# Attention and MLP on one core: 444 matmuls without use behind the last real one

## The chip, the cores and the metric

The kernel runs on one core of one Trainium2 chip. The metric is the device time in microseconds (us) of one execution. Its engines are PE (TensorE, matrix multiply), ACT (ScalarE), DVE (VectorE), POOL (GpSimd) and SP (SyncE, which issues transfers). PEld is PE's loading of weights. SBUF is the on-chip memory of 128 partitions from which operands are read; PSUM holds what PE writes, in eight banks of 512 f32 columns per partition.

## The reference

Windowed attention with 32 global positions, and behind it an MLP with an exact GELU, in f32:

```
s_ll = where(|i - j| <= 32, scale * q_l k_l^T, -1e9);  s_lg = scale * q_l k_g^T
out_l = softmax([s_lg, s_ll]) @ [v_g, v_l]
out_g = softmax(scale * q_g [k_g, k_l]^T) @ [v_g, v_l]
x = concat([out_g, out_l]) as (B * 544, 512)      # B = 8, 8 heads of 64, 512 local positions
h = x @ w_in                                       # 512 x 2048
out = (0.5 * h * (1 + erf(h / sqrt(2)))) @ w_out   # 2048 x 512
```

The output has 4352 rows of 512.

## The kernel before, in words

The 4096 local rows are done in 16 chunks of 256 (a batch element and a half of its positions), and the 256 global rows of all batch elements in a 17th, with the key "g". For each chunk the attention of four pairs of heads comes first, then the MLP of the chunk. So that products come out in f32 accuracy at the faster operand type, an operand is split in a high part (rounded to fp32r) and a low part (the rest), and three matmuls, high by high, low by high and high by low, are added in PSUM.

Names and lines that matter here:

- `wh[n]` and `wl_[n]` are the high and low parts of the weights, 128 x 512 each, for n = 0 to 31: even n is a block of `w_in` (four column blocks of 128, one for each 128 inputs), odd n one of `w_out`. They stay in SBUF. High parts lie two in a tile of 1024 columns, low parts have tiles of their own.
- `st["xh", key, c]` and `st["xl", key, c]` are the parts of the chunk's input, 128 x 256, c = 0 to 3.
- `ml_hc` (lines 709 to 711) makes a hidden block of a chunk: for each c three matmuls with a stationary weight block of 128 x 128 and 256 moving columns, into a PSUM tile of the pool `ps_h`, tag "h", which has two banks.
- `ml_g`, `ml_gh`, `ml_gl` do the GELU (line 279, ACT) and split its result into `gh` and `gl` (lines 132, 134 and 139).
- `ml_o` (lines 744 to 746) multiplies them with `w_out`: three matmuls of 512 moving columns for each block and each of two accumulators.
- `ml_e` and `ml_w` copy an accumulator to SBUF (line 132) and send it out (line 759 for key "g").
- `a_ts`, two SBUF tiles of the attention, and `xs`, the chunk's input before it is split, are free when the last chunk's MLP runs.

The functions don't issue instructions where they stand. They are entered as steps in a list with the engine, the time that it takes and the time that it is due; a planner in the kernel's Python then places the steps engine by engine, and the last loop (line 1086) issues them in that order. `behind` ties each instruction to the one before it on its engine, so the order on an engine is the planner's:

```
    for t, i, x in order:
        x["fn"](x["on"], *x["args"])
        ...
        for y in ins[seen:]:
            if y.engine in last:
                behind(y, last[y.engine])
            last[y.engine] = y.name
```

The program ends when that loop has ended. Its last steps are those of key "g": the matmuls of lines 744 to 746, two copies of the accumulators on ACT, and eight transfers, of which SP's queue issues six and ACT's queue two.

Of the kernel before, what the change touches and what calls it, by code (L numbers as in the profile page):

```python
# [8 lines left out]
F32 = mybir.dt.float32  # L9
# [4 lines left out]
AF = mybir.ActivationFunctionType  # L14
# [70 lines left out]
def attn_mlp(ctx, tc, q_l, k_l, v_l, q_g, k_g, v_g, w_in, w_out, out):  # L85
# [1000 lines left out]
    for t, i, x in order:  # L1086
# [14 lines left out]
            taker[kind] = ins[seen].name, ins[seen].engine  # L1101
        seen = len(ins)


# [1 line left out]
_INS = ['q_l', 'k_l', 'v_l', 'q_g', 'k_g', 'v_g', 'moe_w_in', 'moe_w_out']  # L1106
# [26 lines left out]
```

## Time and profile before

| what | us |
|---|---|
| median of 2 runs | 1052.23 (1052.16 to 1052.3) |
| profiled execution | 1050.12 |
| its span, from the first to the last instruction | 1048.3 |
| PE busy | 1016.1 (97%) |
| ACT busy | 676.9 (65%) |
| DVE busy | 680.4 (65%) |
| POOL busy | 380.4 (36%) |

The granted clock of TensorE is 1.000 on average over the span. The profile is of one execution; its times count from the first instruction. In a row of the timeline stand the start, the duration, the engine, the line of the code, the operation, and the result and operands by their names in the program. A matmul is pipelined: the next one starts long before its record ends, so what a matmul costs in a stream is the step from one start to the next. A row of a group has, behind the count, the sum of the busy time, the mean duration in ns, and the idle time before. A row of windows gives for each engine the busy time and, in brackets, the number of instructions, then the granted clock, the share of the transfer engines that was in use, and GB/s.

### The profile page before, as it was taken

The page shows a single profiled execution, that of the slowest core. Times are in us where ns is not written, and L with a number is a line of the kernel's source. Part 1 is how long each engine was busy: PE and PEld are TensorE (multiplying, and loading weights), DVE is VectorE, ACT ScalarE, POOL GpSimd, SP SyncE. Part 2 cuts the span into 40 slices and gives each one's busy share as a digit, 9 for nine tenths or more (in the row PEclk, how much of TensorE's full clock was granted, in tenths as well). Part 3 has the DMA queues.
Part 4 walks back from the last instruction along what each step waited for, and adds up shares of the span by engine and source line. Part 5 has one row for each costly group of instructions (what it writes and reads, how often), then busy time and mean ns, then how long its engine had stood idle before and what let it go on. Part 6 is the DMA issues. An engine that isn't in the chain of part 4 may idle for free.

```text
span 1048.3 us, 21420 instructions
## 1 busy us (share of the span) xinstructions
PE 1016.1 (97%) x7000; PEld 903.3 (86%) x7000; DVE 680.4 (65%) x2089; ACT 676.9 (65%) x1617; POOL 380.4 (36%) x427
## 2 busy tenths in 40 slices
PE   4989999999999999999999999999999999999998
PEld 2756699998988989998999999998999989999897
DVE  2978968667676768677775777577676777561000
ACT  2978886776667766777575666577565766573221
POOL 2111575243332534334342525244333434243121
PEclk9999999999999999999999999999999999999999
DMA  7785332214221233213322332213322332101000
GB/s 186 226 256 201 55 77 45 53 43 81 49 64 30 42 84 65 59 36 60 82 39 56 61 71 59 61 34 76 64 42 51 64 72 59 44 14 56 1 21 21
DMA packets 277983, 72.29 MB, mean 69 GB/s; under 512 B 263152, under 2 KB 271344, under 8 KB 277872
## 3 DMA queue, kind: packets, MB, share of 16 engines
q1 hardware_dynamic: 271792, 68.57, 28.5%
q10 hardware_dynamic: 6080, 2.36, 0.9%
q8 instruction: 55, 0.90, 0.3%
q14 instruction: 56, 0.46, 0.2%
HBM read 61.41 MB, written 9.44 MB: 68 GB/s over the span
## 4 chain that ended last, share of the span: by engine, by line
PE 84%; DMA 4%; ACT 4%; DVE 3%; SPq 3%; issue 1%; POOL 0%; ACTq 0%; DVEq 0%; POOLq 0%
PE h L709 11%; PE h L711 10%; PE h L710 10%; PE acc L744 10%; PE acc L745 10%; PE acc L746 10%; PE o L517 5%; PE s L406 4%; PE t L480 2%; PE acc L736 2%; PE h L705 2%; PE go L650 2%; ACT a_t L279 1%; PE sg L563 1%; DMA wraw<-in_moe_w_in_dram 1%
## 5 line engine op out<-in xcount | busy, mean ns | idle before, releaser
L139 POOL TENSOR_TENSOR gl<-gf,gh 128x512 fp32r<-128x512 f32 x127 | 167.9, 1322 | 406.4 <-ACT gh L132 282.1
L709 PE MATMUL h<-xh,wh 128*128 128x256 f32 x1024 | 299.1, 292 | 1.4 <-ACT gf L279 1.4
L711 PE MATMUL h<-xh,wl 128*128 128x256 f32 x1024 | 289.7, 283 | 0.0
L710 PE MATMUL h<-xl,wh 128*128 128x256 f32 x1024 | 289.3, 283 | 0.0
L744 PE MATMUL acc<-wh,gh 128*128 128x512 f32 x512 | 206.3, 403 | 0.0
L709 PEld LDWEIGHTS h<-xh,wh 128*128 128x128 f32 x1024 | 195.0, 190 | 10.4 <-ACT gf L279 1.8
L745 PE MATMUL acc<-wh,gl 128*128 128x512 f32 x512 | 201.7, 394 | 0.0
L746 PE MATMUL acc<-wl,gh 128*128 128x512 f32 x512 | 200.6, 392 | 0.0
L710 PEld LDWEIGHTS h<-xl,wh 128*128 128x128 f32 x1024 | 195.2, 191 | 5.7 <-issue 0.7
L711 PEld LDWEIGHTS h<-xh,wl 128*128 128x128 f32 x1024 | 195.0, 190 | 0.0
L279 ACT ACTIVATE gf<-h 128x512 f32<-128x512 f32 x136 | 81.1, 597 | 73.2 <-POOL gl L139 37.7
L279 ACT ACTIVATE a_t<-a_t,sm 128x192 f32<-128x192 f32 (+1 forms) x256 | 116.9, 458 | 2.9 <-DVE sm L431 2.0
L746 PEld LDWEIGHTS acc<-wl,gh 128*128 128x128 f32 x512 | 96.4, 188 | 21.6
L425 DVE CUSTOM_DVE_ANT_0 a_t<-s,mask 128x192 f32<-128x192 f32 (+1 forms) x256 | 80.4, 367 | 48.0 <-PE s L406 48.0
L132 ACT ACTIVATE gh<-gf 128x512 fp32r<-128x512 f32 x95 | 60.0, 632 | 77.2 <-PE acc L746 76.1
L744 PEld LDWEIGHTS acc<-wh,gh 128*128 128x128 f32 x512 | 96.9, 189 | 13.0
L745 PEld LDWEIGHTS acc<-wh,gl 128*128 128x128 f32 x512 | 97.0, 189 | 11.3
L500 DVE TENSOR_TENSOR at<-t,at 128x512 fp32r<-128x512 f32 (+1 forms) x112 | 67.7, 618 | 38.7 <-ACT at L132 38.2
L132 ACT ACTIVATE at<-t 128x512 fp32r<-128x512 f32 (+1 forms) x112 | 59.4, 541 | 49.8 <-PE t L481 25.9
L139 POOL TENSOR_TENSOR vs<-vr,vs 128x512 fp32r<-128x512 f32 x56 | 74.8, 1336 | 42.6 <-DVE vs L134 23.9
L279 ACT ACT_TABLE_LOAD x69 | 88.5, 1283 | 1.2
L548 DVE TENSOR_TENSOR xs<-o,xs 64x256 f32<-64x256 f32 x112 | 46.1, 412 | 51.9 <-ACT xs L543 50.6
(132 smaller groups left out, 1730.9 us busy)
## 6 DMA issues: line engine op xcount, KB each, us to landing
wraw<-in_moe_w_out_dram SPq DMA_DIRECT2D x16, 512.0 KB, 7.6
raws<-in_v_l_dram SPq DMA_DIRECT2D x64, 128.0 KB, 2.5
out_dram<-ob SPq DMA_DIRECT2D x32, 256.0 KB, 2.1
raws<-in_k_l_dram SPq DMA_DIRECT2D x224, 36.0 KB, 1.9
vr<-in_v_l_dram SPq DMA_DIRECT2D x113, 64.0 KB, 2.2
wraw<-in_moe_w_in_dram SPq DMA_DIRECT2D x14, 512.0 KB, 7.4
raws<-in_q_l_dram SPq DMA_DIRECT2D x224, 32.0 KB, 1.8
raws<-in_v_g_dram SPq DMA_DIRECT2D x128, 16.0 KB, 1.9
```

Source lines behind the costliest of these rows:

```text
L132: nc.scalar.activation(out=out, in_=in_, func=AF.Copy)
L139: (nc.vector if e == "v" else nc.gpsimd).tensor_sub(**kw)
L279: nc.scalar.activation(func=func, **kw)
L425: nc.vector.tensor_tensor_reduce(out=a_t[:, j, aoff[half][i]:aoff[half][i] + w], in0=s[:, c:c + w], in1=masks[half][i], scale=1.0, scalar= ...
L500: nc.vector.tensor_sub(out=at[:, 1], in0=st.pop((u, "t", j))[:, :n * P].rearrange("p (n q) -> p n q", q=P), in1=at.bitcast(F32)[:, 0])
L517: nc.tensor.matmul(out=o[:, :, qsl], lhsT=l.rearrange("p s e -> p (s e)"), rhs=r, start=(n == 0), stop=(n == 3), skip_group_check=True)
L709: nc.tensor.matmul(out=h, lhsT=hi, rhs=xh, start=(c == 0 and not (key == (0, 0) and f < HQ and f % 2)), stop=False, skip_group_check=True)
L710: nc.tensor.matmul(out=h, lhsT=hi, rhs=xl, start=False, stop=False, skip_group_check=True)
L711: nc.tensor.matmul(out=h, lhsT=lo, rhs=xh, start=False, stop=(c == NCC - 1), skip_group_check=True)
L744: nc.tensor.matmul(out=acc[t], lhsT=gh[:, f % 2, tsl], rhs=hi, start=(f == 0), stop=False)
L745: nc.tensor.matmul(out=acc[t], lhsT=gl[:, f % 2, tsl], rhs=hi, start=False, stop=False)
L746: nc.tensor.matmul(out=acc[t], lhsT=gh[:, f % 2, tsl], rhs=lo, start=False, stop=(f == NF - 1))
```

## The change

Behind the last loop the changed kernel issues three kinds of instructions more, and ties them to the end of each engine's order in the same way (`after_all`). No line of before is altered, and the order of what stands before is the same.

- `traffic(18)` issues 18 copies of 480 columns on ACT and 18 on DVE, from `xs` into the two tiles of `a_ts`.
- `real(f)`, called four times, issues the twelve matmuls of one hidden block of key "g" once more, into a fresh bank of the pool `ps_h`.
- `run(a, b, n, w, A, B, pre)` issues n equal matmuls into a fresh bank: the stationary block is the 128 columns of B from b on, the moving operand the w columns of A from a on (w is 256 where nothing is given, A the high part of block 2, B the low part of block 3). With `pre` a single matmul with so many columns goes ahead of them.

The calls go through moving operands shifted by 16 columns (and by 4, 8 and 12), stationary blocks shifted by 16 or 32, other pairs of tiles, 512 columns, a single matmul of another width ahead, and other widths. Every matmul starts a new sum, so each overwrites what the one before wrote in its bank, and nothing reads these banks. The output is that of before. The diff:

```diff
+    def after_all(e0):
+        ins = nc.cur_bb.bb.instructions
+        for y in ins[e0:]:
+            if y.engine in last:
+                behind(y, last[y.engine])
+            last[y.engine] = y.name
...
+    def bank(n):
+        return n, ps_h.tile([P, 512], F32, name="z" + next(code), tag="h")
+
+    def mm(t, st_, mv):
+        n = mv.shape[-1]
+        nc.tensor.matmul(out=t[:, 0:n], lhsT=st_, rhs=mv, start=True, stop=True, skip_group_check=True)
+
+    e0 = len(nc.cur_bb.bb.instructions)
+    H = [wh[n] for n in range(2 * NF)]
+    LO = [wl_[n] for n in range(2 * NF)]
+    key = "g"
+    X = [st["xh", key, c] for c in range(NCC)]
+    Y = [st["xl", key, c] for c in range(NCC)]
+    G = st[key, "gh", NF // 2 - 1].rearrange("p a b -> p (a b)")
+
+    def real(f):
+        _, t = bank(0)
+        for c in range(NCC):
+            cs = slice(c * P, c * P + P)
+            mm(t, H[2 * f][:, cs], X[c])
+            mm(t, H[2 * f][:, cs], Y[c])
+            mm(t, LO[2 * f][:, cs], X[c])
+
+    def run(a, b, n=8, w=256, A=None, B=None, pre=0):
+        _, t = bank(0)
+        A = A if A is not None else H[2]
+        B = B if B is not None else LO[3]
+        if pre:
+            mm(t, B[:, 0:P], A[:, 0:pre])
+        for _ in range(n):
+            mm(t, B[:, b:b + P], A[:, a:a + w])
+
+    def traffic(n):
+        for i in range(n):
+            nc.scalar.activation(out=a_ts[0][:, 0, 0:480], in_=xs[:, 0:2].rearrange("p a b -> p (a b)")[:, 0:480], func=AF.Copy)
+            nc.vector.tensor_copy(out=a_ts[1][:, 0, 0:480], in_=xs[:, 2:4].rearrange("p a b -> p (a b)")[:, 0:480])
+
+    traffic(18)
+    real(3)
+    real(4)
+    for a in range(0, 128, 16):
+        run(a, 0, 6)
+    for b in range(0, 128, 32):
+        run(0, b, 4, 512)
+    real(3)
+    real(4)
+    for a in range(0, 128, 16):
+        run(a, 0)
+    for b in range(16, 128, 16):
+        run(0, b, 6)
+    for a in (4, 8, 12):
+        run(a, 0, 6)
+    for A, B in ((H[2], H[0]), (H[2], H[4]), (H[2], H[16]), (LO[3], LO[4]), (LO[3], LO[12]), (LO[3], G), (X[0], H[0]), (X[0], LO[0])):
+        run(0, 0, 6, A=A, B=B)
+    for b in range(0, 128, 16):
+        run(0, b, 5, 512)
+    for p in (16, 32, 48, 64, 80, 96, 112, 128, 160, 192, 224, 512):
+        run(0, 0, 6, pre=p)
+    for w in (64, 128, 192, 320, 384, 448):
+        run(0, 0, 6, w)
+    after_all(e0)
```

More of the change, by code (lines that the diff above doesn't have):

```diff
@@ L1102, in attn_mlp @@
         seen = len(ins)
+    def after_all(e0):
[4 more added lines that the diff above has]
+            last[y.engine] = y.name
+    code = iter([a + b for a in "abcdefghijkmnpqrstuvwxyz" for b in "abcdefghijkmnpqrstuvwxyz"])
+    def bank(n):
[3 more added lines that the diff above has]
+        nc.tensor.matmul(out=t[:, 0:n], lhsT=st_, rhs=mv, start=True, stop=True, skip_group_check=True)
```

## The prediction

> **What bounds the kernel now.** I read the page first, for the span and the engines, then the windows of the last 48 us, then the timeline of the end, because the change only adds work behind what is there.
>
> ```profile
> span 1048.3 us, 21420 instructions
> PE 1016.1 (97%) x7000; PEld 903.3 (86%) x7000; DVE 680.4 (65%) x2089; ACT 676.9 (65%) x1617; POOL 380.4 (36%) x427
> PE 84%; DMA 4%; ACT 4%; DVE 3%; SPq 3%; issue 1%; POOL 0%; ACTq 0%; DVEq 0%; POOLq 0%
> ...
> core 0: us, PE busy (x) PEld busy (x) DVE busy (x) ACT busy (x) POOL busy (x), PEclk, DMA share, GB/s
> 1030.00:1040.00 10.00, 10.00 (x63) 8.94 (x62) 0.04 (x1) 2.46 (x4) 1.29 (x1) 1.00 0.00 0
> 1040.00:1044.00 4.00, 3.98 (x18) 2.97 (x16) 0.65 (x1) 0.60 (x1) 0.00 (x0) 1.00 0.00 0
> 1044.00:1048.30 4.30, 0.00 (x0) 0.00 (x0) 0.00 (x0) 0.60 (x1) 0.00 (x0) 0.97 0.46 122
> ```
>
> TensorE (PE) is the bound: it is busy for 97% of the span, holds 84% of the chain that ends last, and in the last stage before 1044 it has no idle time at a granted clock of 1.00. Every matmul has its own weight load (7000 of each). Only the last 4.3 us are not PE's: one copy and the output's transfers. So what is put behind the last matmul on PE lengthens the span by its whole length, less the part of those 4.3 us that it covers.
>
> The end, instruction by instruction (start, duration, engine, line):
>
> ```profile
> 1039.73 0.39 PE L744 MATMUL acc<-wh,gh 128*128 128x512 f32 x1
> ...
> 1043.36 0.39 PE L745 MATMUL acc<-wh,gl 128*128 128x512 f32 x1
> 1043.59 0.39 PE L746 MATMUL acc<-wl,gh 128*128 128x512 f32 x1
> ...
> 1044.01 0.60 ACT L132 ACTIVATE ob<-acc 128x512 f32<-128x512 f32 x1 [0.76 <-PE acc L746]
> 1044.64 0.87 ACTq L759 DMA_DIRECT2D out_dram<-ob  x2
> ...
> L759 SPq DMA_DIRECT2D out_dram<-ob x6: 342/416/443, 1043.3 to 1045.6; - x6
> out_dram<-ob SPq DMA_DIRECT2D x6, 64.0 KB, 1.8
> ```
>
> The last matmul starts at 1043.59 and ends at 1043.98; 0.03 us later ScalarE (ACT) copies the accumulator, and two queues send it out. The last issue on SP's queue starts at 1045.6 and lands 1.8 us later, at 1047.4. The remaining 0.9 us to 1048.3 are the closing of the program.
>
> **The change part by part.** Nothing is removed or moved. PE gets 444 matmuls, counted from the calls in the diff. Of 256 columns there are 24 + 24 in the four calls of real, 48 in the first run over a, 64 in the second, 42 in the second run over b, 18 at a = 4, 8, 12, 48 with other operands, and 72 behind the short first matmuls: 340. Of 512 columns there are 16 + 40 + 1: 57. Of 320, 384 and 448 there are 6 each: 18. Narrower ones are 18 of 64 to 192 and 11 of 16 to 224: 29. ACT and VectorE (DVE) get 18 copies of 480 columns each.
>
> *What a matmul costs in a stream* is the step from start to start, not the duration, since matmuls overlap. For 512 columns the rows above give it: from 1039.73 to 1043.59 there are 17 steps, 3.86 / 17 = 0.227 us. For 256 columns, and for others:
>
> ```profile
> 1037.28 0.28 PE L709 MATMUL h<-xh,wh 128*128 128x256 f32 x1
> ...
> 1038.23 0.28 PE L711 MATMUL h<-xh,wl 128*128 128x256 f32 x1
> 1038.35 0.40 PE L744 MATMUL acc<-wh,gh 128*128 128x512 f32 x1
> 1038.58 0.40 PE L745 MATMUL acc<-wh,gl 128*128 128x512 f32 x1
> 1038.82 0.39 PE L746 MATMUL acc<-wl,gh 128*128 128x512 f32 x1
> ...
> 743.51 0.44 PE L563 MATMUL sg<-k,gs 128*128 128x288 f32 x2
> 743.79 0.39 PE L744 MATMUL acc<-wh,gh 128*128 128x512 f32 x1
> ...
> 907.74 0.38 PE L480 MATMUL t<-ident,a_t 128*128 128x128 f32 x2
> ...
> 907.96 0.27 PE L481 MATMUL t<-ident,ge 128*128 128x128 f32 x1
> ```
>
> Nine matmuls of 256 columns run from 1037.28 to 1038.35, 0.119 us each; I take 0.12. Two of 288 take 0.28 us together, 0.14 each, between the two sizes as a line through 0.12 and 0.23 would have it. Two of 128 columns take 0.22 us, 0.11 each: below 256 columns a matmul hardly gets cheaper. On that line 320, 384 and 448 columns are estimates of 0.148, 0.175 and 0.203 us; for the 29 narrow ones I take 0.11.
>
> The sum on PE: 340 x 0.12 = 40.8; 57 x 0.227 = 12.9; 6 x (0.148 + 0.175 + 0.203) = 3.2; 29 x 0.11 = 3.2; together 60.1 us.
>
> [...]
>
> *The seam.* On PE the new rows stand directly behind the last real matmul; zaa, zab, zac are the new accumulator banks, taken in turn from the two that h used:
>
> ```order
>  L745 MATMUL acc_13646<-wh,gl 128x512
>  L746 MATMUL acc_13646<-wl,gh 128x512
> -L1128 UNCONDITIONAL_BRANCH
> +L1118 MATMUL zaa<-xh,wh 128x256
> +L1118 MATMUL zaa<-xl,wh 128x256
> +L1118 MATMUL zaa<-xh,wl 128x256
> ```
>
> The first has no wait but one on PE itself, for the bank's earlier matmuls, which ended before 1039 (the rows of h above). So the first new matmul starts one step behind 1043.59, at 1043.82.
>
> On DVE, as on ACT, the copies stand behind the last real instruction:
>
> ```order
>  L139 TENSOR_TENSOR gl<-gf,gh 128x512
> -L1128 UNCONDITIONAL_BRANCH
> +L1148 COPY a_t_122<-xs 128x480 x18
> +L1199 UNCONDITIONAL_BRANCH
> ```
>
> *The copies* I cost at nothing. The nearest rows:
>
> ```profile
> L134 DVE COPY ao<-t 128x512 f32<-128x512 f32 x5 | 3.4, 684 | 1.5 <-PE t L483 1.5
> L132 ACT ACTIVATE ob<-acc 128x512 f32<-128x512 f32 x34 | 19.0, 596 | 11.0 <-PE acc L746 9.9 <-PE o L517 0.6
> 1039.96 0.69 DVE L139 TENSOR_TENSOR gl<-gf,gh 128x512 fp32r<-128x512 f32 x1 [44.27 <-ACT gh L132]
> ```
>
> DVE is free from 1040.65, and 18 x 0.68 = 12.3 us end at 1053. ACT is free when its two transfers are issued, at 1045.51, and 18 x 0.60 = 10.7 us end at 1056.2. Both are long over when PE ends, and no matmul waits for them. The output's copy and its transfers stand ahead of ACT's copies, so they are not delayed. Were PE's cover gone, the copies would set an end near 1057. Beside PE they can cost at most what other engines' work costs it: with an ACT instruction running, 512 columns stepped 0.23 to 0.24 (1038.35 to 1038.82) against 0.227 in the quiet end, 5% of the 20 us or so that lie beside copies, 1 us; I take none.
>
> *The end.* 1043.82 + 60.1 = 1103.9, the end of the last matmul 0.16 us behind (as 1043.98 is behind 1043.82), then the closing, 0.9: a span of 1105.0, which is 56.7 us more than 1048.3. The transfers of the output, over at 1047.4, are covered. The profiled execution took 1050.12 us, 1.8 more than its span; it would take 1106.8. The median of the two runs is 1052.23, 2.1 us above the profiled one; with 56.7 it is **1108.9 us**, 5.4% more.
>
> *Bounds.* Below: no full-height matmul of the rows steps faster than 0.11; with that for 256 columns the sum falls by 3.4 us, and with nothing for the closing by 0.9: 1104.6. Above: shifted places are not in the trace; 18 matmuls (a = 4, 8, 12) lie off the multiples of 16 columns that all else keeps, and at twice their step they add 2.2. With 0.24 for 512 columns 0.7 is added; with 0.05 us of wait at each of the 68 changes of bank 3.4; with the copies' 1 us the time is 1116. I take the middle rows because the kernel's own operands, at many different places, all step alike.
>
> **The rivals.**
>
> *Shifted operands are slow.* Outside the 18 above, 98 matmuls of 256 columns have a moving operand shifted by multiples of 16 columns, 42 of 256 and 47 of 512 a shifted weight block. If every shifted one took twice its step, as plain f32 takes longer in
>
> ```profile
> L705 PE MATMUL h<-xf,wf 128*128 128x256 f32 x128 | 32.5, 388 | 2.2 <-DVE xf L134 1.0 <-ACT gf L279 0.8 <-ACT xf L132 0.2
> ```
>
> (0.39 us against 0.28), that is 158 x 0.12 + 47 x 0.227 = 29.6 us: 1138. Against it: real operands start at several column blocks and tiles and show no such steps. For it: none of them starts inside a block. 0.05.
>
> *A wait at each bank.* All 68 new tiles begin with a wait on PE itself. Two banks alternate, so the wait is for the tile before the last, whose last matmul ended four to eight steps, 0.4 us or more, earlier. Were it for the last tile, each would cost the tail of a matmul (0.28 - 0.12), the hop of 0.03 and a weight load of 0.19:
>
> ```profile
> L710 PEld LDWEIGHTS h<-xl,wh 128*128 128x128 f32 x1024 | 195.2, 191 | 5.7 <-issue 0.7
> ```
>
> 0.38 x 68 = 26 us: 1135. 0.05.
>
> *The clock falls.* In the window 1044.00:1048.30 PE is idle throughout and the granted clock is still 0.97 on average, so it falls, if at all, some 4 us after PE stops. At the seam PE stops for nothing. Were all 60 us at half clock, the time would be 1169. 0.02. [...]
>
> *Not slower: the matmuls do not run.* Nobody reads their banks. If what compiles or loads the program dropped them, the copies would be all that is left: 1056.2 + 0.9 = 1057.1, 8.8 us more, 1061.0, which is within 2%. It decides only if PE's addition falls below 25 us (2% is 21.0 us, and 4.3 - 0.9 - 0.2 are given back at the end), 0.056 us for each matmul, half of the fastest step above. Against it: the new rows stand in PE's order of the built program. 0.02.
>
> **How the numbers follow.** The forecast has 0.86, with 1104 to 1116 as its own range. The slow rivals have 0.12 together, and partial forms of them begin just above it; the rival that is not slower has 0.02, of which I give a quarter to an end that is faster by something no row shows. I take 1103 to 1116, which leaves out about 0.15. About 2%, 21 us, is what a measurement of this kernel can tell from no change. Slower: 0.98; within: 0.015; faster: 0.005.
>
> **What would show it.** In the profile of the changed kernel: PE rows of L1118 from 1043.8 on without idle time; steps of 0.12 and 0.227 in groups of like operands; copies over before 1060; the last matmul near 1104 and a span of 1105; the clock at 1.00 until then. Groups at shifted places that step at 0.2 would show the first rival, idle PE at the head of each tile the second, PEclk of 0.5 the third, no rows of L1118 on PE the last. A stream that steps below 0.11 would put the time below the range.

## The result, and the profile after

The changed kernel took 1108.76 us (two runs, 1107.18 and 1110.34) against 1052.23: a ratio of 1.0537, with a 95% interval of 1.0473 to 1.0602. In a second series, four runs beside 17 of before, it took 1108.11 against 1052.05, a ratio of 1.0533 (1.0518 to 1.0549). The profiled execution is the one of 1110.34.

The page of the changed kernel, its first lines and the granted clock in 40 slices:

```profile
span 1108.6 us, 22345 instructions
PE 1078.5 (97%) x7444; PEld 962.5 (87%) x7444; DVE 687.7 (62%) x2107; ACT 688.3 (62%) x1635; POOL 381.1 (34%) x427
PEclk9999999999989999999999999999999999999999
```

PE has 444 matmuls more and stays at 97% of a longer span. One slice of the clock, the twelfth, is lower; more of that below.

The timeline of PE at the seam, and the stretch from the first new matmul to the end of the last step (columns as in the prediction's windows):

```profile
1047.20 0.39 PE L745 MATMUL acc<-wh,gl 128*128 128x512 f32 x1
1047.42 0.39 PE L746 MATMUL acc<-wl,gh 128*128 128x512 f32 x1
1047.65 0.28 PE L1118 MATMUL zaa<-xh,wh 128*128 128x256 f32 x1
1047.76 0.28 PE L1118 MATMUL zaa<-xl,wh 128*128 128x256 f32 x1
...
1047.65:1107.51 59.86, 59.86 (x445) 57.09 (x443) 4.38 (x11) 11.51 (x19) 0.00 (x0) 1.00 0.04 10
```

The first new matmul starts 0.23 us behind the last real one, and PE is then busy for all of 59.86 us at a clock of 1.00. The prediction's sum for this stretch was 60.1.

What is not as predicted in this execution is where the seam lies: the last real matmul starts at 1047.42, and before it was 1043.59. Nothing was added ahead of it. The windows of both kernels around the lower slice, before first:

```profile
310.00:315.00 5.00, 2.96 (x23) 2.41 (x21) 4.29 (x15) 4.92 (x16) 0.00 (x0) 1.00 0.37 60
315.00:320.00 5.00, 4.35 (x32) 4.19 (x33) 3.85 (x12) 4.92 (x8) 1.29 (x1) 1.00 0.26 41
```

and after:

```profile
310.00:315.00 5.00, 3.07 (x24) 2.52 (x22) 4.29 (x15) 4.93 (x17) 0.00 (x0) 0.97 0.34 55
315.00:320.00 5.00, 4.24 (x20) 4.24 (x21) 3.85 (x12) 4.91 (x9) 1.28 (x1) 0.50 0.29 47
320.00:325.00 5.00, 5.00 (x26) 4.48 (x26) 1.40 (x4) 2.68 (x5) 0.62 (x1) 0.85 0.26 53
```

From 314.7 to 321.5 the clock is at half, and PE does 20 matmuls between 315 and 320 where it did 32. The same instructions are late by 0.1 us at 312, by 2.7 at 319.6, and by 3.8 at the seam. So 2.6 us of the delay belong to the low clock. The rest came at a clock of 1.00, in jumps of about half a us near 490, 610 and 840 us, with one back near 730; their cause is open.

### The profile page after: what moved, and what is told of

It is laid out like the page before. It is cut to its first block, busy times and chain, and to the rows that moved or that the text cites. A ratio compares the mean times of both kernels' runs of the same rounds, so it can differ in the third digit from the quotient of the medians.

```text
span 1108.6 us, 22345 instructions
## 1 busy us (share of the span) xinstructions
PE 1078.5 (97%) x7444; PEld 962.5 (87%) x7444; DVE 687.7 (62%) x2107; ACT 688.3 (62%) x1635; POOL 381.1 (34%) x427
## 4 chain that ended last, share of the span: by engine, by line
PE 82%; ACT 5%; DMA 4%; DVE 4%; SPq 3%; issue 1%; POOL 1%; ACTq 0%; DVEq 0%; POOLq 0%
PE h L709 10%; PE h L711 10%; PE h L710 10%; PE acc L744 9%; PE acc L745 9%; PE acc L746 9%; PE o L517 4%; PE s L406 4%; PE t L480 2%; PE acc L736 2%; PE go L650 2%; PE h L705 2%; ACT a_t L279 1%; PE sg L563 1%; ACT L279 1%
```

## The experiments

Four questions were open after the result. Does the stream cost what it takes, or did errors cancel? What would the rivals have cost? Do shifted places matter at all? And why did the real part of the kernel end later?

**Copies alone.** The body of the change is cut to its first call:

```diff
     traffic(18)
-    real(3)
-    ...
-        run(0, 0, 6, w)
     after_all(e0)
```

> The 444 matmuls are left out, the 18 copies on each of the two engines stay. This is what the rival that is not slower would leave. The prediction's price for it was 1061.0 (a span of 1057.1). The trace of the changed kernel now has the copies' own steps: on ACT from 1050.4 to 1061.3 in 17 steps, 0.64 us each, from 3.0 us behind the start of the last real matmul; in the kernel before that would be 1046.6 + 18 x 0.64 = 1058.1, and 0.9 for the closing makes a span of 1059.0, 10.7 more than before: 1062.9. Theory: the copies alone set the end there, and lengthen nothing ahead of it: 1061 to 1064, and the last real matmul keeps its place relative to the rows before it. Rival, copies slow the matmuls that they lie beside: over 1066.

It took 1060.79 us (1059.30 to 1062.33), a ratio of 1.0082 (1.0066 to 1.0099). Its ACT copies, with the shortest, median and longest duration and the first and last start:

```profile
L1147 ACT ACTIVATE a_t<-xs x18: 602/602/604, 1046.0 to 1056.8; 128x480 f32<-128x480 f32 x18
```

The first starts 2 us behind the last real matmul (1044.08), not 3 us as in the changed kernel, so the expectation was 1 us too late at that point. The time is 0.2 us below the 1061 to 1064 that were expected. The last copy ends at 1057.4, and the span of 1058.3 ends 0.8 behind it. The prediction's price for the rival that is not slower, 1061.0, holds to 0.2 us, in part by luck: in this profile the copies end 1.2 us later than its 1056.2. The last real matmuls still step at 0.227, with DVE's copies beside them from 1041.1 on, so the copies slowed nothing ahead of ACT's.

**The stream twice.** Behind the list stands the whole list once more, without the copies:

```diff
         run(0, 0, 6, w)
+    real(3)
+    ...
+        run(0, 0, 6, w)
     after_all(e0)
```

> The stream of 444 matmuls is issued twice, the copies once. Theory: PE's stream lies bare on the path, so a second one costs what the first took from start to end in its trace, 59.9 us (1047.65 to 1107.3 and one step), and the 3.3 us of tail that the first one covered aren't given back again: 1108.8 + 59.9 = 1168.7, within 2. Rival, part of the first stream was hidden beside copies and transfers: the second costs more than the first, over 1171. Rival, the first holds a start-up cost: under 1166.

It took 1168.25 us, 60.1 more than the changed kernel in the same series (1108.11). The two streams in its windows:

```profile
1044.16:1104.02 59.86, 59.86 (x445) 57.28 (x444) 4.39 (x11) 11.50 (x19) 0.00 (x0) 1.00 0.04 10
1104.02:1163.88 59.86, 59.86 (x445) 57.10 (x443) 0.00 (x0) 0.00 (x0) 0.00 (x0) 1.00 0.00 1
```

The first has the copies (4.39 us on DVE, 11.5 on ACT) and the output's transfers beside it, the second has nothing, and both take 59.86 us, the 57 matmuls of 512 columns 13.19 us in each. So the copies cost PE nothing, the stream has no start-up cost, and the 3.5 us of the tail are given back once. Here the seam is at 1044.16, near the predicted 1043.82.

**A wait at the seam.**

```diff
-    traffic(18)
+    for i in range(18):
+        nc.scalar.activation(out=X[0], in_=xs[:, 0], func=AF.Copy)
```

> The copies are replaced by 18 on ACT that write a moving operand of the first new matmuls (its own value once more), so PE has to wait at the seam for them: ACT is free 2 us behind PE's end, 18 steps of some 0.45 us make 8 us, so PE stands idle for about 10 us. The 444 matmuls follow unchanged. It prices the prediction's rival of the falling clock. Theory, from the profiles: the clock falls 4.1 us behind PE's end (before: PE ends at 1043.98, half clock from 1048.08), comes back 3.4 or 6.8 us after work has begun again (the two lengths that the profiles show), and costs half of that, 1.7 to 3.4 us; the first 256-column matmuls step at 0.21, the rest at 0.12. The stream then takes 61.6 to 63.3 from its start, and the time is 1118 to 1122. Rival, the clock stays low for the whole stream: over 1165. Rival, it comes back at once: the stream takes 59.9, 1117.

It took 1122.83 us (one run). The timeline and the windows around the wait:

```profile
1047.90 0.39 PE L746 MATMUL acc<-wl,gh 128*128 128x512 f32 x1
1057.98 0.58 PE L1118 MATMUL zaa<-xh,wh 128*128 128x256 f32 x1 [9.69 <-ACT xh L1151]
1058.35 0.42 PE L1118 MATMUL zaa<-xl,wh 128*128 128x256 f32 x1
1058.57 0.42 PE L1118 MATMUL zaa<-xh,wl 128*128 128x256 f32 x1
...
1052.00:1056.00 4.00, 0.00 (x0) 0.00 (x0) 0.00 (x0) 3.71 (x10) 0.00 (x0) 0.56 0.00 0
1056.00:1060.00 4.00, 2.02 (x9) 2.03 (x10) 0.00 (x0) 1.79 (x5) 0.00 (x0) 0.50 0.01 4
1060.00:1064.00 4.00, 4.00 (x26) 4.00 (x25) 0.00 (x0) 0.00 (x0) 0.00 (x0) 0.66 0.00 0
```

PE stands idle for 9.69 us. The mean of 0.56 puts the fall of the clock at 1052.5, 4.2 us behind PE's end, and that of 0.66 puts its return at 1062.7, 4.7 us after work began again. In between, 256 columns step at 0.21 to 0.22. The stream takes 62.0 us instead of 59.86, so the clock costs 2.2 us here and not 60: the rival of a low clock for the whole stream falls even where PE does stop. The time lies 0.8 us over the expectation because the real part of this execution ended 4.3 us later than in the profile before, with the clock at half for 6.8 us at 62.6 and again at 315.2 (in the changed kernel once, at 314.7).

**A bank for each matmul.**

```diff
-    traffic(18)
-    ...
+    for i in range(10):
+        run(0, 0, 12)
+    for i in range(120):
+        run(0, 0, 1)
+    for i in range(60):
+        run(0, 0, 2)
+    for i in range(40):
+        run(0, 0, 3)
```

> Instead of the 444 matmuls, 480 of 256 columns with the same operands and no copies: 10 banks of 12, then 120 banks of one, 60 banks of two, 40 banks of three. It prices the wait at each change of bank. Theory: the wait is for the tile before the last, so a tile of n may start (n - 1) x 0.12 + 0.28 + 0.03 + L behind the start of the tile two before it, with L the time from a released wait to the start of a matmul, some 0.2: steps of 0.12 in the tiles of 12, 0.25 for each matmul alone in its bank, 0.16 in twos, 0.12 to 0.13 in threes. Rival, the wait is for the last tile: 0.5, 0.31 and 0.25. Rival, a wait costs nothing at all: 0.12 throughout.

It took 1119.60 us (one run). The four stretches, of 120 matmuls each:

```profile
1044.59:1058.98 14.39, 14.39 (x121) 14.39 (x120) 0.00 (x0) 0.60 (x1) 0.00 (x0) 1.00 0.15 38
1058.98:1085.53 26.55, 26.55 (x123) 18.61 (x121) 0.00 (x0) 0.00 (x0) 0.00 (x0) 1.00 0.00 1
1085.53:1102.37 16.84, 16.84 (x121) 16.25 (x121) 0.00 (x0) 0.00 (x0) 0.00 (x0) 1.00 0.00 1
1102.37:1116.77 14.40, 14.40 (x122) 14.35 (x120) 0.00 (x0) 0.00 (x0) 0.00 (x0) 1.00 0.00 1
```

Divided by 120 these are steps of 0.120 with twelve matmuls in a bank, 0.221 with one, 0.140 with two and 0.120 with three. That is the order of the theory (0.12, 0.25, 0.16, 0.12 to 0.13) and far from the rival's 0.5, 0.31 and 0.25. The wait exists. It is for the tile before the last, since a step of 0.221 is shorter than the 0.28 that one matmul lasts; by the theory's sum L comes out at 0.13 us, from the ones and the twos alike, and not 0.2. From three matmuls in a bank on the wait is covered. The change has four at least.

**Narrower weights.** In the rows of before a step is 0.11 us at 128 columns and 0.119 at 256; the floor that is meant below is the 0.11. The matmul itself is written with m stationary columns, so this part of the list is

```diff
+            nc.tensor.matmul(out=t[0:m, 0:w], lhsT=LO[3][:, 0:m], rhs=H[2][:, 0:w], start=True, stop=True, skip_group_check=True)
...
+    for m in (128, 64, 32):
+        for w in (64, 128, 192, 256, 320, 384, 448, 512):
+            cols(m, w)
```

> Instead of the 444 matmuls, real(3) and real(4) and then groups of 16 equal matmuls with 128, 64 and 32 stationary columns (so the weight load is shorter, and the result has so many partitions), each at 64, 128, 192, 256, 320, 384, 448 and 512 moving columns. [...] Theory B, a fixed cost of each matmul: the floor falls, but 256 columns stay at 0.119 and 512 at 0.23. Theory C, PE's issue of two instructions sets the floor: 64 and 128 columns stay at 0.11 with any weights.

It took 1104.16 us (one run). Groups of 16 in the timeline; the step is the difference between the starts of two rows, divided by 16:

```profile
1052.89 2.10 PE L1153 MATMUL zaf<-wh,wl 128*128 128x256 f32 x16
1054.82 2.51 PE L1153 MATMUL zag<-wh,wl 128*128 128x320 f32 x16
...
1063.25 3.83 PE L1153 MATMUL zaj<-wh,wl 128*128 128x512 f32 x16
1066.92 1.07 PE L1153 MATMUL zak<-wh,wl 128*64 128x64 f32 x16
1067.83 1.15 PE L1153 MATMUL zam<-wh,wl 128*64 128x128 f32 x16
1068.82 1.58 PE L1153 MATMUL zan<-wh,wl 128*64 128x192 f32 x16
```

With 128 stationary columns, 256 moving ones step at 0.121 (1052.89 to 1054.82), and 64 to 192 at 0.107 to 0.114. With 64 stationary columns, 64 moving ones step at 0.057 and 128 at 0.062: the floor falls to about half, so it goes with the stationary columns, as B had it, and C falls. (The result's partitions shrink along with the weights, so that the weight load alone makes the floor is not shown.) But 256 columns only fall from 0.121 to about 0.114, and 320 (0.146) and 512 (0.23) stay within 1% of what they were. B falls as well as it was put: 512 columns stay, as it had it, but 256 get cheaper by some 0.007 us, so what is left beside the floor is not the same for all widths. What makes it up is open.

**Odd places.** Instead of the list:

```diff
+    for a in (0, 1, 2, 3, 5, 6, 7, 9, 33, 101):
+        run(a, 0, 12)
+    for b in (0, 1, 2, 3, 5, 6, 7, 9, 33, 101):
+        run(0, b, 12)
+    for a, b in ((1, 1), (2, 1), (3, 3), (33, 101)):
+        run(a, b, 12)
+    for b in (0, 128, 256):
+        run(b, b, 12, A=H[2], B=H[2])
```

> Instead of the 444 matmuls, real(3) and real(4) and then groups of 12 equal matmuls of 256 columns with the moving operand shifted by 0, 1, 2, 3, 5, 6, 7, 9, 33 and 101 columns, the same for the stationary block, four with both shifted, and three with both operands in the same tile, overlapping. In the changed kernel all shifts were multiples of 4. Theory: the place doesn't matter, steps of 0.113 to 0.124 in all groups. Rival, places that are no multiple of 4 columns (16 bytes) are read in more pieces: 0.15 to 0.24 there. Rival, the two operands get in each other's way when they overlap: over 0.13 in the last three groups.

It took 1089.18 us (one run). Some of its 27 groups of twelve, again with the step as the difference of starts: first no shift, the moving operand shifted by 1, 2 and 3, and the start of the next group; then the three at the end with both operands in one tile:

```profile
1047.65 1.60 PE L1118 MATMUL zac<-wh,wl 128*128 128x256 f32 x12
1049.09 1.63 PE L1118 MATMUL zad<-wh,wl 128*128 128x256 f32 x12
1050.55 1.57 PE L1118 MATMUL zae<-wh,wl 128*128 128x256 f32 x12
1051.96 1.56 PE L1118 MATMUL zaf<-wh,wl 128*128 128x256 f32 x12
1053.36 1.63 PE L1118 MATMUL zag<-wh,wl 128*128 128x256 f32 x12
...
1082.00 1.60 PE L1118 MATMUL zbc<-wh 128*128 128x256 f32 x12
1083.44 1.60 PE L1118 MATMUL zbd<-wh 128*128 128x256 f32 x12
1084.88 1.60 PE L1118 MATMUL zbe<-wh 128*128 128x256 f32 x12
```

Without a shift a group takes 1.44 us, 0.120 a step; shifted by 1 column 1.46, by 2 columns 1.41, by 3 columns 1.40; in one tile 1.44. Over all groups the mean step lies between 0.116 and 0.122. Both rivals fall: no place costs more than about 2%.

**A gap filled.** The kernel before, with nothing at its end, and one place in `st_t` altered:

```diff
         ge = st[u, "ge"]
+        if u == (2, 1, 0) and j == 0:
+            for n in range(12):
+                nc.tensor.matmul(out=t[:, 0:256], lhsT=wh[2][:, 0:P], rhs=wh[2][:, 0:256], start=True, stop=True, skip_group_check=True)
         for n, c in enumerate(own(half)):
```

> The kernel before, with 12 matmuls of 256 columns of no use put ahead of the transposes that PE waits for at 311.9 to 313.4 us, into the bank that the transposes overwrite; nothing at the end. In the changed kernel's profile the clock was at half from 314.7 to 321.5, behind two stretches of idle PE (1.54 and 1.15 us), and the real part of the kernel ended 3.8 us later than in the profile before. Theory: the idle stretches open it, in some executions and not in others, and work in the first of them (12 x 0.12 = 1.4 us, which fits in 1.54) keeps the clock at 1.00: every execution near the profiled one of before, 1050.1, and a median 1 to 2 us under before's. Rival: the half clock has another cause, and the executions scatter as before's do, 1050 to 1053. Rival: the added matmuls make the transposes late: 1 us above before's.

It took 1049.41 us (12 runs, 1048.43 to 1051.64) against 1052.05 (17 runs, 1048.84 to 1053.86): a ratio of 0.9981, 0.9971 to 0.9991. Its windows at the place:

```profile
310.00:315.00 5.00, 4.90 (x41) 4.59 (x40) 4.26 (x15) 4.92 (x19) 0.00 (x0) 1.00 0.29 59
315.00:320.00 5.00, 3.85 (x32) 3.61 (x31) 4.16 (x11) 4.93 (x7) 1.30 (x1) 1.00 0.35 58
```

PE is now busy for 4.90 of the first 5 us, and the clock stays at 1.00. With twelve matmuls that compute nothing the median is 2.6 us lower. The expectation that every execution would be near 1050.1 was too strong: in the profiled one, of 1051.64, the clock fell at another place, from 57.0 to 60.4. Nor is the clock the whole of the scatter, since one execution with a mean clock of 1.000 took 1051.38. It is most of it before: there the three executions with a clock of 1.000 took 1048.84, 1049.96 and 1050.09, and the ten with 0.997 or less took 1051.77 to 1053.86. By the means, the gain is 2.0 us, and the mean clock rises from 0.9976 to 0.9986, which is about 1.0 us of the span. So by the recorded clocks about half of the gain is the clock's, and the cause of the rest is open.

**The changed kernel once more.**

> The changed kernel once more, in five rounds beside before, for the scatter: its two executions were 1107.18 and 1110.34, those of before 1052.16, 1052.30 and 1050.12 (profiled). Theory: the stream at the end costs 56.4 us each time (59.9, less 3.5 of the tail), and what scatters is the clock in the real part: executions 56 to 57 above before's at the same clock, from 1106.5 on, and the difference of the medians 56 to 58. Rival: the added instructions lengthen the real part as such: every execution at 1107 or above, and none within 1 us of 1106.5.

Its executions took 1108.38, 1107.71, 1109.07 and 1107.84 us, at mean clocks of 0.997 and 0.998, so none was undisturbed. The difference of the medians is 56.1 us. In its profiled execution (1108.38) the last real matmul starts at 1045.47 and the stream takes the same 59.86 us from 1045.69, with the clock at half for 3.4 us at 60.1 and again at 316.1. That the added instructions lengthen the real part as such is not excluded by these four, none of which came within 1 us of 1106.5; but with a bank for each matmul, 480 matmuls stand behind the real part, the granted clock is 1.000, and the last real matmul starts at 1044.36, 0.77 us behind before's. Of these 0.77 us 0.66 are there already at 100 us; from there to the seam the same instructions take 0.1 us more than before. That speaks against it.

## Why the prediction was right

*What bounds the kernel.* PE at the end, with nothing to hide behind: right. The stream lies bare on the path (twice the stream, twice 59.86).

*The sum on PE.* Forecast 60.1, measured 59.86. By the start-to-start steps of the changed kernel: 340 matmuls of 256 columns took 40.9 us (forecast 40.8), 57 of 512 took 13.2 (12.9), 18 of 320 to 448 took 3.2 (3.2), 29 narrower ones took 2.6 (3.2). The step of 512 columns was 0.231 and not 0.227, because I read it from the last seventeen rows, which step lower than most. That they are quiet isn't the reason: the 57 step at 0.231 in the second stream of the experiment too, with nothing beside them. The 2.6 for the narrow ones misleads, as the groups with a single narrow matmul (here of 16, 32, 192 and 224 columns) ahead of six of 256 show:

```profile
1092.33 0.99 PE L1118 MATMUL zcc<-wh,wl 128*128 128x16 f32 x7
1093.16 0.99 PE L1118 MATMUL zcd<-wh,wl 128*128 128x32 f32 x7
...
1099.76 0.98 PE L1118 MATMUL zcm<-wh,wl 128*128 128x192 f32 x7
1100.58 0.98 PE L1118 MATMUL zcn<-wh,wl 128*128 128x224 f32 x7
```

From start to start a group takes 0.82 to 0.83 us whatever the width of the single one, and six of 256 take 0.71 (0.118 each, the mean of the 268 in groups without a single matmul ahead). So each single costs about 0.11, as forecast: one of 16 columns steps 0.027 itself, but the matmul behind it steps 0.204. Counted so, the narrow ones took 3.2 and the 340 took 40.2: they step at 0.118, and I had rounded 0.119 up to 0.12. The misses are 0.3 us too little for 512 columns and 0.6 too much for 256, and they cancel in part.

*The seam.* No idle time, a step of 0.23: right. *The copies* cost PE nothing: right, shown by the equal streams. Their own steps were off: 0.45 us on DVE (forecast 0.68) and 0.64 on ACT (0.60), which didn't matter behind PE's cover. One sign that the prediction named did not come: the copies were not over before 1060 in the profile but at 1061.9, since the seam was late and the issue of ACT's two transfers took 1.89 us where it had taken 0.87. *The end:* the closing behind PE's last matmul is 0.885 us in seven of the kernels, forecast 0.9.

*The median.* 56.7 us more were forecast, 56.5 and 56.1 measured. But that 1108.9 met 1108.76 to 0.1 us is partly luck: single executions lie 3.2 us apart, and the medians of before hold the same disturbance as those of after. The forecast carried it over as the 2.1 us between before's profile and its median without naming it. It is for the most part the half clock in the real part, and the profile before, with a clock of 1.000 throughout, could not show it. Nor is 2% the least that can be told from no change, as the prediction put it: the copies alone made 0.8% and the filled gap 0.2%, both clear of the scatter.

*The rivals.* Slow places: none found (0.116 to 0.122 at any place tried). A wait at each bank: it exists for one or two matmuls in a bank, at 0.10 and 0.02 us a matmul, and no longer for three (a step of 0.120). The clock: at the seam PE didn't stop, and it stayed at 1.00; where PE was made to stop, it cost 2.2 us, so the rival's 1169 was far too high, since it let the clock stay low for 60 us. Not slower: the matmuls ran, and the price, 1061.0, was measured as 1060.8.

## What to carry to other kernels

Work added to the engine that has no idle time costs its whole length (here 59.86 us, and 59.86 once more), and its step is best read from start to start in rows of the same kind, over whole groups, not from durations: a short step of a narrow matmul can be paid back by the one behind it (0.027 us and then 0.204). The tail that it covers, 3.5 us here, is given back only once. A kernel's own scatter can come from a low clock far from any change (here from 314.7 to 321.5, worth 2.6 us at a seam that lies 730 us later), so compare where the instructions ahead of the change lie before explaining the difference by the change.

## What the runs showed of the hardware that was not expected

The granted clock fell to half without PE being idle for long. In the profiles it stayed there for 3.41 us (the filled gap, 57.0 to 60.4), 6.83 (the changed kernel, 314.7 to 321.5) and 10.24 (the wait at the seam, with PE idle for 9.69 us, 1052.5 to 1062.7). PE's busy time in the 3.41 us ahead of such a fall, in the changed kernel (first row) and in the kernel with the filled gap (second, at the other place):

```profile
311.28:314.69 3.41, 1.79 (x13) 1.24 (x11) 3.20 (x11) 3.39 (x13) 0.00 (x0) 1.00 0.31 49
53.55:56.97 3.42, 1.67 (x11) 1.08 (x9) 3.37 (x14) 0.13 (x1) 0.71 (x1) 1.00 0.90 204
```

PE was busy for about half of each, and its longest single idle stretch in the first was 1.54 us. In the other falls inside a kernel's real part it was busy for 1.1 to 1.7 us of the 3.41. Behind the same two gaps the clock fell in some of the profiled executions and not in all. Before's profile has them too, and PE is busy for less of the same stretch there:

```profile
311.28:314.69 3.41, 1.68 (x12) 1.13 (x11) 3.21 (x11) 3.39 (x13) 0.00 (x0) 1.00 0.31 50
```

Its clock stayed at 1.00, in this stretch and in the 10 us from 315 on. So how long PE works in the 3.41 us ahead (1.68 us without a fall, 1.79 with one) didn't tell by itself whether the clock fell. What did is open.

Useless matmuls can be worth more than nothing: with twelve of them, 1.4 us in a gap of 1.54, the kernel was 0.19% faster (0.09 to 0.29%), though by the recorded clocks only about half of that is the clock's.
